# A decode block that streams 561 MB: the output projection's weights as one tile behind the last K load

## The chip, the core and the metric

The kernel runs on one core of a Trainium2 chip. A core has engines that each work through their own list of instructions: TensorE (PE: matmuls, with weight loads shown apart as PEld), VectorE (DVE), ScalarE (ACT), GpSimd (POOL) and SyncE (SP). SyncE issues the transfers from HBM into the on-chip memory SBUF. Matmul results land in PSUM. An instruction waits until those it depends on have signalled, and whatever stands behind it in the same engine's list waits with it. The metric is the device time of one execution in microseconds; smaller is better.

## What is computed

One decoding step for two sequences (B = 2): layer norm, attention against a cache, a residual, and an MLP behind a second layer norm.

```python
q = (layernorm(x) @ wq)                               # 2 x 512 -> 32 heads x 128
scores = einsum("bhqd,bhkd->bhqk", q, k_cache) * 128 ** -0.5
p = softmax(scores)                                   # over 8192 positions
o = einsum("bhqk,bhkd->bhqd", p, v_cache)             # 32 heads x 128
h = x + o.reshape(2, 4096) @ wo                       # wo: 4096 x 512
out = h + gelu(layernorm(h) @ w1 + b1) @ w2 + b2      # w1: 512 x 1792
```

All is float32. The caches k and v are 2 x 32 x 8192 x 128 each, 268 MB each; wq and wo are 8.4 MB, W1 and W2 3.67 MB each.

## The kernel before

The heads are worked off in units. Units 0 to 29 are a pair of heads (a group g = 0 to 14) of one sequence b; units 30 and 31 are heads 30 and 31, each for both sequences. In the text K5 and V5 are the loads of unit 5's keys and values, 8.39 MB each. In a pair's unit, the first head's 8192 positions lie on partitions 0 to 63 and the second's on 64 to 127, 128 positions a partition, so one partition's row in HBM is 64 KB. K30, K31 and V30 come as two loads, one a sequence, and V31 as four.

All of these, wq at the start and the MLP's weights at the end (`wt`) share three slots of 64 KB a partition (`slot()`, the pool `kv`, the tile `kv` in the profile). A load can be issued when the slot's last user is done. The order of the loads is wq, K0, K1, V0, K2, V1, K3 and so on, so a K is two transfers ahead of its use.

For a unit, in four chunks of 32 positions a partition: VectorE multiplies the chunk by q (`multiply`, L183, 128 x 4096), GpSimd adds the upper half of each row to the lower (`halve`, L187, chunks 0 to 2), VectorE sums what is left (`add_up`, L190). `row_max` (L200 or L198) takes the maximum of a partition, TensorE turns it into a row (L202), `all_max` (L207) takes the maximum over a row and matmuls (L211) give it to all partitions. ScalarE's `exps` (L229, L223) writes the probabilities. `values` (L260) multiplies them with V into the PSUM tile `so`, by turns in four groups of rows; `gather` (L266) copies it out and `head_sum` (L274, L276) adds the four groups. A float32 matmul shows as two records.

The output projection runs along with the groups. `load_wo(g)` (L171) loads the group's 256 rows of wo, 0.52 MB in rows of 4 KB a partition, into one of two buffers of the tile `wog`. In the next group's second unit `head_out` scales the pair's result into the tile `orow` with two VectorE operations (L282), `turn` transposes it by two matmuls (L292), `turned` copies it (L296) and adds its product with the group's wo into the PSUM tile `rowacc` by two matmuls (L299). Heads 30 and 31 have their wo rows in a tile of their own and come last: head 30 by `project` (L303); head 31's part is kept apart, and its effect on the layer norm and on the output is computed from `wl`, its 128 rows of wo.

The end, behind V31: the MLP's weights W1 (`w1t`, L372, four loads) and W2 (`w2t`, L376, six loads) go to the slot `wt`. The layer norm's parts are prepared from `rowacc` while V31 is still arriving (L400 to L418); then come V31's matmuls, `gather`, the last head's part (L438, L442), W1's matmuls (L453), the variance (L458), the activation (L468, L470), a transpose (L473), W2's matmuls (L476), a copy (L479) and the store (L480).

The instructions are written in Python's order and a scheduler places them on the engines' lists; it also adds the waits. `behind(m)` is the program's way to say that an engine's next instructions stand behind the instruction m on that engine. Transfers use eight completion semaphores in turn, so that a load may wait for an older one that used the same. Fifteen tiny loads of b1 into the tile `mark` (L321) are spread among the loads of units 24 and on: each waits for the one before.

Of the kernel before, what the change touches and what calls it, by code (L numbers as in the profile page):

```python
# [21 lines left out]
LH = 2  # L22
WARM = 3
MARKS = 15


@with_exitstack
def tile_decode_block(ctx: ExitStack, tc: tile.TileContext, x, k, v, wq, wo, w1, b1, w2, b2, out):
    nc = tc.nc
    B, H, SK, DH = k.shape  # L30
    D = x.shape[-1]
    F = w1.shape[1]
    DC = D // P
# [21 lines left out]
    def slot():  # L55
        return kv.tile([P, ROW], F32, name="kv", tag="kv")
# [41 lines left out]
    y2 = wts.tile([B, D], F32, name="y2", tag="wog")  # L98
# [38 lines left out]
    for j in range(QW // 512):  # L137
        nc.scalar.activation(q2[:, j * 512:(j + 1) * 512], so2[j], AF.Copy)

    QP, S, MX, MT, GM, LT, RL, SS, OP, OT, TP, WO = ({} for _ in range(12))  # L140

    def make_q(g):
        QP[g] = psq.tile([P, B, DH], F32, name="qps")
# [9 lines left out]
    def load(src, i, parts):  # L153
        g, b = units[i]
        h = heads[g][0]
        t = slot()
        if b is not None:
            nc.sync.dma_start(t, src[b, h:h + 2].rearrange("h (p j) d -> (h p) (j d)", j=NS2))
            return t
        tv = t.rearrange("p (b j d) -> p b j d", b=B, d=DH)  # L160
        for e in range(B):
            for s0, n in parts[e]:
                nc.sync.dma_start(tv[:, e, s0:s0 + n],
                                  src[e, h].rearrange("(p j) d -> p j d", j=NS1)[:, s0:s0 + n])
        return t

    def load_wo(g):
        t = wts.tile([P, 2, D], F32, name="wog", tag="wog")
        h = heads[g][0]
        if g < NP:  # L170
            nc.sync.dma_start(t, wo[h * DH:(h + 2) * DH, :].rearrange("(p r) n -> p r n", r=2))  # L171
        else:
            nc.sync.dma_start(t, wo[h * DH:, :].rearrange("(h p) n -> p h n", p=P))
        WO[g] = t

    def chunk(t, c):
        return t[:, c * CH * DH:(c + 1) * CH * DH].rearrange("p (j d) -> p j d", d=DH)
# [11 lines left out]
    def add_up(i, c, t, n):  # L189
        nc.vector.tensor_reduce(S[i][:, c * CH:(c + 1) * CH], chunk(t, c)[:, :, 0:n], axis=AX.X, op=ALU.add)  # L190

    def row_max(i):
        g, b = units[i]
        if not b:
            MX[g] = work.tile([P, B], F32, name="mx")
            MT[g] = psm.tile([1, B, P], F32, name="sm")
        if b is None:
            nc.vector.tensor_reduce(MX[g], S[i].rearrange("p (b j) -> p b j", b=B), axis=AX.X, op=ALU.max)  # L198
# [49 lines left out]
    def values(i, t, e=None):  # L248
        g, b = units[i]
        so = so2[g % 2]  # L250
        if b is not None:
            nu, at, w, cols = NS2 // 4, 0, 16, slice(0, 16)
            p = ptz[b]
        else:
            b, nu, w = e, NS1 // 4, 8
            at, cols = b * nu, ((slice(8, 16), slice(0, 8))[b])
            p = ptz[b][:, nu * (g - NP):nu * (g - NP + 1), :]
        for u in range(nu):
            n = u % NG
            m = nc.tensor.matmul(so[32 * n:32 * n + w], p[:, u, cols], t[:, (at + u) * 512:(at + u + 1) * 512],  # L260
                                 start=(b == 0 and u < NG), stop=(b == B - 1 and u >= nu - NG))
# [16 lines left out]
    def head_out(g):  # L278
        op, rl = OP.pop(g), RL.pop(g)
        if g < NP:  # L280
            for e in range(2):
                m = nc.vector.tensor_scalar(orow[:, :, e * HP:(e + 1) * HP].rearrange("m r p -> m p r"),  # L282
                                            op.rearrange("m (p r) -> m p r", r=2), rl[:, e:e + 1], None,
                                            op0=ALU.mult)
# [4 lines left out]
    def turn(g):  # L289
        TP[g] = psm.tile([P, 2, B], F32, name="sm")  # L290
        for r in range(2):
            nc.tensor.matmul(TP[g][:, r, :], orow[:, r, :], bmask, start=True, stop=True)  # L292

    def turned(g):
        t = work.tile([P, 2, B], F32, name="ot2")
        m = nc.vector.tensor_copy(t, TP.pop(g))  # L296
        w = WO.pop(g)
        for r in range(2):
            nc.tensor.matmul(rowacc, t[:, r, :], w[:, r, :], start=(g == 0 and r == 0), stop=False)  # L299
        return m  # L300

    def project(g):
        nc.tensor.matmul(rowacc, OT.pop(g), WO[NP][:, g - NP, :], start=False, stop=(g == GL - 1))  # L303

    def behind(m):
        return tc.issue_after(m.ins) if m is not None else nullcontext()

    whole = [[(0, NS1)], [(0, NS1)]]
    KT, VT = {0: load(k, 0, whole)}, {}
    first = None  # L310
    for i, (g, b) in enumerate(units):
        if i >= 1:
            VT[i - 1] = load(v, i - 1, whole)
        if i + 1 < NU:
            KT[i + 1] = load(k, i + 1, whole)
        if b == 0 or i == NU - 2:
            load_wo(g)
        if i == NU - 8 and MARKS:
            mark = const.tile([16, 32], F32, name="mark")
            for n in range(1, MARKS + 1):  # L320
                nc.sync.dma_start(mark[:n, :n + 8], b1[:n * 32].rearrange("(p c) -> p c", p=n)[:, :n + 8])  # L321
        kt = KT.pop(i)
        S[i] = work.tile([P, NS2], F32, name="s", bufs=3)
        out_of = g - 1 if b == 1 else NP - 1 if i == NU - 1 else -1
        for c in range(NCH):
            with behind(first):
                m = multiply(i, c, kt)
            first = None
            if c < NCH - 1:
                halve(c, kt)  # L330
            with behind(m):
                if c == 0:
                    if b != 1 and g >= 1:
                        inverse(g - 1)
                    if out_of >= 0:
                        first = head_out(out_of)
                        turn(out_of)
                elif c == 1:
                    if out_of >= 0:
                        first = turned(out_of)  # L340
# [4 lines left out]
            if c == 2 and b == 0 and i >= 1 or c == 2 and i == NU - 2:  # L345
                values(i - 1, VT.pop(i - 1))
                gather(g - 1)
                head_sum(g - 1)
            if c == 2 and i == NU - 1:
                values(i - 1, VT[i - 1], 0)  # L350
        add_up(i, NCH - 1, kt, DH)
        row_max(i)
        if b != 0:
            first = all_max(g)
            exps(g)
            total(g)
        if b == 1:
            values(i - 1, VT.pop(i - 1))
# [9 lines left out]
        nc.sync.dma_start(b2s[e:e + 1], b2[None, :])  # L368
    w1t = wt[:, 0:DC * F].rearrange("p (c f) -> p c f", c=DC)
    w1v = w1.rearrange("(p c) f -> p c f", c=DC)  # L370
    for c in range(DC):
        nc.sync.dma_start(w1t[:, c], w1v[:, c])  # L372
    w2t = wt[:, DC * F:2 * DC * F].rearrange("p (t d) -> p t d", t=FT)
    w2v = w2.rearrange("(p t) d -> p t d", t=FT)
    for t, n in ((0, 4), (4, 4), (8, 2), (10, 2), (12, 1), (13, 1)):
        nc.sync.dma_start(w2t[:, t:t + n, :], w2v[:, t:t + n, :])  # L376

    inverse(GL)
    junk = const.tile([P, 2], F32, name="junk")
    nc.scalar.activation(junk[:, 0:1], LT[GL][:, 0:1], AF.Sqrt)  # L380
    values(NU - 2, VT.pop(NU - 2), 1)
    gather(GL - 1)
    head_sum(GL - 1)
    head_out(GL - 1)
# [6 lines left out]
        at[0] += n  # L391
        return late[:parts, at[0] - n:at[0]]

    wl = WO[NP][:, LH - 1, :]
# [112 lines left out]
```

## Time and profile before

| | |
|---|---|
| time, median of 3 runs | 1316.67 us (1316.04 to 1317.26) |
| the profiled execution, its own time | 1316.34 us |
| its span, first to last instruction | 1314.2 us |
| moved from HBM | 561.02 MB, 427 GB/s over the span |
| busy share of the span | DVE 72%, PE 35%, POOL 33%, ACT 4% |
| mean granted TensorE clock | 0.648 of full speed |

The profile's page cuts the span into 40 slices of 32.9 us and gives for each the busy tenths of each engine, the granted TensorE clock and the bytes moved. A group of instructions is shown by the line, the engine, the operation and the tiles it writes and reads (`kv<-kv,qps`), with its count, busy time, mean time, the idle time ahead of it and what ended that. The chain of waits follows the work that ended last backwards, at each step to what released it. "SPq" rows are issues of transfers by SyncE; a wait row reads "who waited <- for whom: us in total, times, longest".

### The profile page before, as it was taken

What the parts mean: (1) busy time and instruction counts of PE and PEld (TensorE: products, weight loads), DVE (VectorE), ACT (ScalarE), POOL (GpSimd) and SP (SyncE); (2) the same over time, 40 slices, a digit from 0 to 9 for tenths busy, and PEclk for the clock granted to TensorE, in tenths of its full rate; (3) what the DMA queues carried; (4) which work ended last, traced back from release to release, by engine and by line L of the source; (5) the groups of instructions that cost most, each with busy time, mean ns of one, the idle gap of its engine ahead of it and who ended that gap; (6) DMA issues with size and microseconds to landing.
All of it is one profiled execution on the core that took longest, in us unless ns stands there. A gap on an engine that the chain in (4) does not pass through costs nothing.

```text
span 1314.2 us, 6813 instructions
## 1 busy us (share of the span) xinstructions
PE 459.7 (35%) x2829; PEld 148.8 (11%) x2829; DVE 950.5 (72%) x426; ACT 52.3 (4%) x173; POOL 436.6 (33%) x108
## 2 busy tenths in 40 slices
PE   3006133431443324233431343324233431343357
PEld 0001011100111011011100111011011100111113
DVE  1799667688676788767688676788767688669761
ACT  0001000000000000000000000000000000000001
POOL 0444422244422344422244422344422344424230
PEclk9557566575666657666675666656666675666668
DMA  9999999999999999999999999999999999999996
GB/s 415 431 447 409 430 437 435 425 437 431 439 433 423 432 439 428 433 433 431 435 431 431 437 431 433 433 435 427 435 431 429 439 426 436 435 431 432 421 425 266
DMA packets 14403, 561.46 MB, mean 427 GB/s; under 512 B 1809, under 2 KB 1825, under 8 KB 5157
## 3 DMA queue, kind: packets, MB, share of 16 engines
q1 hardware_dynamic: 14368, 561.03, 99.1%
q8 instruction: 22, 0.36, 0.1%
q14 instruction: 9, 0.07, 0.0%
q10 hardware_dynamic: 4, 0.00, 0.0%
HBM read 561.02 MB, written 0.00 MB: 427 GB/s over the span
## 4 chain that ended last, share of the span: by engine, by line
DMA 52%; DVE 28%; PE 13%; issue 3%; ACT 1%; POOL 1%; SPq 0%; DVEq 0%; ACTq 0%
DMA kv<-in_A_k_cache_dram 33%; DMA mark<-in_B_b_dram 17%; DVE kv L183 15%; DVE s L190 11%; PE so L260 11%; DMA kv<-in_A_v_cache_dram 2%; POOL kv L187 1%; PE sm L211 1%; ACT pt L229 1%; DVE orow L282 1%; DVE gm L207 0%; PE sm L202 0%; PE so L453 0%; DVE mx L200 0%; PE po L476 0%
## 5 line engine op out<-in xcount | busy, mean ns | idle before, releaser
L183 DVE TENSOR_TENSOR kv<-kv,qps 128x4096 f32<-128x4096 f32 x128 | 563.7, 4406 | 303.7 <-DMA kv<-in_A_k_cache_dram 294.1
L187 POOL TENSOR_TENSOR kv<-kv 128x2048 f32<-128x2048 f32 x96 | 433.7, 4525 | 828.8 <-DVE kv L183 494.3
L260 PE MATMUL so<-kv,pt 128*16 128x512 f32 (+1 forms) x2048 | 305.5, 734 | 275.6 <-DMA kv<-in_A_v_cache_dram 255.0
L190 DVE TENSOR_REDUCE s<-kv 128x32 f32<-128x2048 f32 (+1 forms) x128 | 356.7, 2806 | 5.9 <-POOL kv L187 5.5
L260 PEld LDWEIGHTS so<-kv,pt 128*16 128x16 f32 (+1 forms) x2048 | 77.2, 111 | 468.2 <-DMA kv<-in_A_v_cache_dram 270.6
L292 PE MATMUL sm<-bmask,orow 4*128 4x2 f32 x60 | 15.1, 352 | 190.5 <-DVE orow L282 190.5
L147 PE MATMUL qps<-q,pick 2*64 2x128 f32 x136 | 18.0, 411 | 150.5 <-DVE kv L183 150.5
L299 PE MATMUL rowacc<-wog,ot 128*2 128x512 f32 x60 | 53.0, 1037 | 49.6 <-DVE ot L296 49.6
L202 PE MATMUL sm<-ident,mx 128*1 128x128 f32 x34 | 10.7, 326 | 135.8 <-DVE mx L200 127.9
L292 PEld LDWEIGHTS sm<-bmask,orow 4*128 4x128 f32 x60 | 13.8, 317 | 193.3 <-DVE orow L282 178.8
L147 PEld LDWEIGHTS qps<-q,pick 2*64 2x64 f32 x136 | 11.8, 203 | 175.9 <-DVE kv L183 157.5
L266 ACT ACTIVATE ss<-so 128x512 f32<-128x512 f32 x17 | 10.1, 597 | 539.9 <-PE so L260 539.9
L216 ACT ACTIVATE nb<-sm 128x2 f32<-128x2 f32 x17 | 2.9, 172 | 675.9 <-PE sm L211 675.9
L229 ACT ACTIVATE pt<-s,nb 64x128 f32<-64x128 f32 x60 | 23.9, 399 | 1.2
L211 PE MATMUL sm<-gm,srow 1*128 1x2 f32 x68 | 16.7, 347 | 8.6 <-DVE gm L207 8.6
L274 PE MATMUL sm<-ss,sel 128*4 128x128 f32 x120 | 15.6, 273 | 10.9 <-ACT ss L266 10.9
L202 PEld LDWEIGHTS sm<-ident,mx 128*1 128x1 f32 x34 | 2.5, 79 | 146.3 <-DVE mx L200 134.3
L207 DVE TENSOR_REDUCE gm<-sm 1x4 f32<-1x256 f32 (+1 forms) x17 | 7.0, 412 | 16.1 <-PE sm L202 16.1
L211 PEld LDWEIGHTS sm<-gm,srow 1*128 1x128 f32 x68 | 15.3, 309 | 13.8 <-DVE gm L207 13.8
L134 PE MATMUL so<-kv,yT 128*2 128x512 f32 x64 | 9.4, 751 | 17.2 <-DMA kv<-in_A_wq_dram 17.2
L299 PEld LDWEIGHTS rowacc<-wog,ot 128*2 128x2 f32 x60 | 5.1, 104 | 72.6 <-DVE ot L296 50.9
L274 PEld LDWEIGHTS sm<-ss,sel 128*4 128x4 f32 x120 | 9.3, 87 | 26.7 <-ACT ss L266 24.7
(98 smaller groups left out, 104.5 us busy)
## 6 DMA issues: line engine op xcount, KB each, us to landing
kv<-in_A_k_cache_dram SPq DMA_DIRECT2D x4, 4096.0 KB
kv<-in_A_v_cache_dram SPq DMA_DIRECT2D x3, 4096.0 KB
wog<-in_A_wo_dram SPq DMA_DIRECT2D x16, 512.0 KB
kv<-in_B_w_dram SPq DMA_DIRECT2D x4, 896.0 KB
kv<-in_A_v_cache_dram SPq DMA_DIRECT2D x1, 2048.0 KB
kv<-in_B_w_dram SPq DMA_DIRECT2D x2, 1024.0 KB
kv<-in_A_v_cache_dram SPq DMA_DIRECT2D x1, 1536.0 KB
kv<-in_B_w_dram SPq DMA_DIRECT2D x2, 512.0 KB
```

The costliest lines, as they stand in the source:

```text
L147: nc.tensor.matmul(QP[g][s * HP:(s + 1) * HP, b], pick[32 * n:32 * n + B, b, :], q2[32 * n:32 * n + B, at:at + DH], start=True, stop=True)
L183: return nc.vector.tensor_tensor(kc, kc, QP[g][:, b, None, :].to_broadcast([P, CH, DH]), op=ALU.mult)
L187: nc.gpsimd.tensor_tensor(kc[:, :, 0:HP], kc[:, :, 0:HP], kc[:, :, HP:DH], op=ALU.add)
L190: nc.vector.tensor_reduce(S[i][:, c * CH:(c + 1) * CH], chunk(t, c)[:, :, 0:n], axis=AX.X, op=ALU.add)
L202: nc.tensor.transpose(MT[g][:, e, :], MX[g][:, e:e + 1], ident)
L211: nc.tensor.matmul(GM[g], srow[:, s, :], gm[:, :, s % n], start=(s == 0), stop=(s == 1))
L229: nc.scalar.activation(ptz[b][q, :, 4 * m:4 * m + 4], s[q], AF.Exp, bias=nb[q, b:b + 1], scale=SCALE, accum_out=lt4[q, m:m + 1])
L260: m = nc.tensor.matmul(so[32 * n:32 * n + w], p[:, u, cols], t[:, (at + u) * 512:(at + u + 1) * 512], start=(b == 0 and u < NG), stop=(b = ...
L274: nc.tensor.matmul(OP[g], sel4[:, :, j], sj, start=(j == 0), stop=(j == 3))
L282: m = nc.vector.tensor_scalar(orow[:, :, e * HP:(e + 1) * HP].rearrange("m r p -> m p r"), op.rearrange("m (p r) -> m p r", r=2), rl[:, e: ...
L292: nc.tensor.matmul(TP[g][:, r, :], orow[:, r, :], bmask, start=True, stop=True)
L299: nc.tensor.matmul(rowacc, t[:, r, :], w[:, r, :], start=(g == 0 and r == 0), stop=False)
```

## The change

wo's rows for heads 0 to 29 are no longer loaded with each group. One load, issued behind K31, brings all 3840 of them as one tile of 7.86 MB (60 KB a partition, in three rows of 20 KB) into one of the three slots; head 30's and 31's rows follow in a tile of their own, `wol`. The results of five groups (ten heads) are kept in `orow`, now laid out per group, and turned together: `turn(j)` makes ten matmuls and `turned(j)` one copy into `oall`, after groups 4, 9 and 14. `project_all` then multiplies all of `oall` with the tile in 30 matmuls, spread over four groups of rows of `so`, gathers them with one copy, and adds them into `rowacc` with one matmul. It is placed in the last unit's third chunk, and the last unit's `row_max` is put behind it on TensorE.

Beside that: K0 comes in two loads of 4.19 MB, W1 in two instead of four, W2 in four (8, 4, 1 and 1 of its 14 parts) instead of six. V30's first half is multiplied after the last unit's softmax, with the second half, and not inside the unit. `add_up` is put behind the multiply of the next chunk. The marks are issued with units 18 to 22, three to a unit.

```diff
@@ tiles @@
-    wts = ctx.enter_context(tc.tile_pool(name="wts", bufs=2))
+    wts = ctx.enter_context(tc.tile_pool(name="wts", bufs=1))
-    orow = const.tile([4, 2, P], F32, name="orow")
-    nc.gpsimd.memset(orow, 0.0)
+    orow = const.tile([4, GP, 2, DH], F32, name="orow")
+    oall = const.tile([P, NP // GP, 2 * GP, B], F32, name="oall")
@@ loads @@
-            nc.sync.dma_start(t, src[b, h:h + 2].rearrange("h (p j) d -> (h p) (j d)", j=NS2))
+            rows = src[b, h:h + 2].rearrange("h (p j) d -> (h p) (j d)", j=NS2)
+            for s0, n in parts:
+                nc.sync.dma_start(t[:, s0 * DH:(s0 + n) * DH], rows[:, s0 * DH:(s0 + n) * DH])
-    def load_wo(g):
...
+    def load_wo():
+        t = slot()
+        tv = t[:, 0:NP * 2 * D].rearrange("p (j c) -> p j c", c=2 * GP * D)
+        nc.sync.dma_start(tv, wo[0:HL * DH, :].rearrange("(j p r) n -> p j (r n)", p=P, r=2 * GP))
+        return tv.rearrange("p j (r n) -> p j r n", n=D)
+
+    def load_last():
+        t = wts.tile([P, LH, D], F32, name="wol", tag="wol")
+        nc.sync.dma_start(t, wo[HL * DH:, :].rearrange("(h p) n -> p h n", p=P))
+        return t
@@ output projection @@
-            for e in range(2):
-                m = nc.vector.tensor_scalar(orow[:, :, e * HP:(e + 1) * HP].rearrange("m r p -> m p r"),
-                                            op.rearrange("m (p r) -> m p r", r=2), rl[:, e:e + 1], None,
-                                            op0=ALU.mult)
-            return m
+            return nc.vector.tensor_tensor(orow[:, g % GP], op[:, None, :].to_broadcast([4, 2, DH]),
+                                           rl[:, :, None].to_broadcast([4, 2, DH]), op=ALU.mult)
+    def turn(j):
+        rows = orow.rearrange("m k e d -> m (k e d)").rearrange("m (p r) -> m r p", r=2 * GP)
+        TP[j] = psm.tile([P, 2 * GP, B], F32, name="sm")
+        for r in range(2 * GP):
+            nc.tensor.matmul(TP[j][:, r, :], rows[:, r, :], bmask, start=True, stop=True)
+
+    def turned(j):
+        return nc.vector.tensor_copy(oall[:, j], TP.pop(j))
+
+    def project_all(wot):
+        so, n = so2[(NP - 1) % 2], 2 * NP
+        for q in range(n):
+            j, r = divmod(q, 2 * GP)
+            m = nc.tensor.matmul(so[32 * (q % NG):32 * (q % NG) + B], oall[:, j, r, :], wot[:, j, r, :],
+                                 start=(q < NG), stop=(q >= n - NG))
+        gather(NP - 1)
+        nc.tensor.matmul(rowacc, sel[:, :B], SS.pop(NP - 1), start=True, stop=False)
+        return m
@@ units @@
-    KT, VT = {0: load(k, 0, whole)}, {}
+    KT, VT = {0: load(k, 0, [(0, NS2 // 2), (NS2 // 2, NS2 // 2)])}, {}
...
+        if i == NU - 2:
+            wot = load_wo()
+            wol = load_last()
+        at = i - (NU - 14)
+        if 0 <= at < 5:
+            for n in range(3 * at + 1, 3 * at + 4):
+                nc.sync.dma_start(mark[:n, :n + 8], b1[:n * 32].rearrange("(p c) -> p c", p=n)[:, :n + 8])
...
             if c >= 1:
-                add_up(i, c - 1, kt, HP)
+                with behind(m):
+                    add_up(i, c - 1, kt, HP)
...
             if c == 2 and i == NU - 1:
-                values(i - 1, VT[i - 1], 0)
+                last = project_all(wot)
         add_up(i, NCH - 1, kt, DH)
-        row_max(i)
+        with behind(last):
+            row_max(i)
@@ end @@
-    for c in range(DC):
-        nc.sync.dma_start(w1t[:, c], w1v[:, c])
+    for c in range(0, DC, 2):
+        nc.sync.dma_start(w1t[:, c:c + 2], w1v[:, c:c + 2])
-    for t, n in ((0, 4), (4, 4), (8, 2), (10, 2), (12, 1), (13, 1)):
+    for t, n in ((0, 8), (8, 4), (12, 1), (13, 1)):
-    values(NU - 2, VT.pop(NU - 2), 1)
+    vt = VT.pop(NU - 2)
+    values(NU - 2, vt, 0)
+    values(NU - 2, vt, 1)
```

More of the change, by code (lines that the diff above doesn't have):

```diff
@@ L97, in tile_decode_block @@
     nc.vector.reciprocal(rs, sd)
-    y2 = wts.tile([B, D], F32, name="y2", tag="wog")
+    y2 = wts.tile([B, D], F32, name="y2", tag="wol")
     nc.vector.tensor_scalar(y2, x2, mv[:, 0:1], rs, op0=ALU.subtract, op1=ALU.mult)
@@ L138, in tile_decode_block @@
         nc.scalar.activation(q2[:, j * 512:(j + 1) * 512], so2[j], AF.Copy)
-    QP, S, MX, MT, GM, LT, RL, SS, OP, OT, TP, WO = ({} for _ in range(12))
+    QP, S, MX, MT, GM, LT, RL, SS, OP, OT, TP = ({} for _ in range(11))
     def make_q(g):
@@ L286, in head_out @@
         OT[g] = work.tile([P, B], F32, name="ot") if g < GL else otz[:, 0:32:16]
         nc.vector.tensor_tensor(OT[g], op, rl, op=ALU.mult)
[L289 to L299, printed above, removed]
+    def turn(j):
[3 more added lines that the diff above has]
+            nc.tensor.matmul(TP[j][:, r, :], rows[:, r, :], bmask, start=True, stop=True)
@@ L300, in turned @@
         return m
     def project(g):
-        nc.tensor.matmul(rowacc, OT.pop(g), WO[NP][:, g - NP, :], start=False, stop=(g == GL - 1))
+        nc.tensor.matmul(rowacc, OT.pop(g), wol[:, g - NP, :], start=False, stop=(g == GL - 1))
     def behind(m):
         return tc.issue_after(m.ins) if m is not None else nullcontext()
-    whole = [[(0, NS1)], [(0, NS1)]]
-    KT, VT = {0: load(k, 0, whole)}, {}
-    first = None
+    whole, full = [[(0, NS1)], [(0, NS1)]], [(0, NS2)]
+    assert NS2 == NCH * CH
@@ L311, in tile_decode_block @@
+    KT, VT = {0: load(k, 0, [(0, NS2 // 2), (NS2 // 2, NS2 // 2)])}, {}
+    mark = const.tile([16, 32], F32, name="mark")
+    first = last = None
     for i, (g, b) in enumerate(units):
         if i >= 1:
-            VT[i - 1] = load(v, i - 1, whole)
+            VT[i - 1] = load(v, i - 1, full if i <= 2 * NP else whole)
         if i + 1 < NU:
[L315 to L320, printed above, removed]
+            KT[i + 1] = load(k, i + 1, full if i + 1 < 2 * NP else whole)
+        if i == NU - 2:
[4 more added lines that the diff above has]
+            for n in range(3 * at + 1, 3 * at + 4):
@@ L336, in tile_decode_block @@
                         first = head_out(out_of)
-                        turn(out_of)
+                        if out_of >= 0 and out_of % GP == GP - 1:
+                            turn(out_of // GP)
                 elif c == 1:
-                    if out_of >= 0:
-                        first = turned(out_of)
+                    if out_of >= 0 and out_of % GP == GP - 1:
+                        first = turned(out_of // GP)
                     if b != 0 and g < GL:
@@ L343, in tile_decode_block @@
             if c >= 1:
-                add_up(i, c - 1, kt, HP)
-            if c == 2 and b == 0 and i >= 1 or c == 2 and i == NU - 2:
+                with behind(m):
+                    add_up(i, c - 1, kt, HP)
+            if c == 2 and (b == 0 and i >= 1 or i == NU - 2):
                 values(i - 1, VT.pop(i - 1))
```

10 lines of the change are left out of this document (2 added, 8 removed).

## The prediction

> **What bounds the kernel now.** The page first: the span, the moved bytes by slice, the queue, and the chain of waits by engine.
>
> ```profile
> span 1314.2 us, 6813 instructions
> ...
> DMA  9999999999999999999999999999999999999996
> GB/s 415 431 447 409 430 437 435 425 437 431 439 433 423 432 439 428 433 433 431 435 431 431 437 431 433 433 435 427 435 431 429 439 426 436 435 431 432 421 425 266
> ...
> q1 hardware_dynamic: 14368, 561.03, 99.1%
> ...
> DMA 52%; DVE 28%; PE 13%; issue 3%; ACT 1%; POOL 1%; SPq 0%; DVEq 0%; ACTq 0%
> ```
>
> 561 MB on one queue, in nines to the last slice: the kernel is a stream, and 561.03 MB at the middle's 433 GB/s would be 1296 us. What is above that is lost at the ends: the slice with 409, and the last one with 266. So next come the stages by time (columns: busy us and count by engine, granted TensorE clock, DMA share, GB/s).
>
> ```profile
> 98.60:131.40 32.80, 20.13 (x135) 6.43 (x135) 30.39 (x14) 3.42 (x10) 13.67 (x3) 0.73 0.97 410
> 580.00:740.00 160.00, 53.11 (x320) 16.97 (x320) 119.46 (x51) 5.46 (x20) 54.42 (x13) 0.65 1.01 434
> 1288.00:1300.00 12.00, 11.31 (x88) 4.62 (x80) 0.55 (x2) 0.60 (x1) 0.00 (x0) 0.90 0.99 407
> 1302.00:1304.00 2.00, 2.00 (x15) 0.47 (x11) 0.16 (x1) 1.72 (x3) 0.00 (x0) 0.50 0.52 204
> 1304.00:1306.00 2.00, 2.00 (x19) 0.50 (x11) 0.54 (x1) 0.00 (x0) 0.00 (x0) 0.98 0.13 49
> 1308.00:1314.20 6.20, 3.14 (x112) 2.87 (x109) 0.29 (x1) 0.00 (x0) 0.00 (x0) 1.00 0.02 3
> ```
>
> The last weights move between 1304 and 1306; I put the landing of the last W2 piece at 1305.3. The span ends 9 us later. The chain of waits in its last stretch (start, us, what) says why:
>
> ```profile
> 1199.60 28.52 DMA kv<-in_A_v_cache_dram
> ...
> 1228.16 9.19 PE so L260 x64
> ...
> 1239.82 4.33 DVE kv L183
> ...
> 1272.19 0.19 DVE mx L198
> ...
> 1276.19 5.59 PE so L260 x32
> ...
> 1287.59 8.45 PE so L260 x64
> ...
> 1300.46 1.37 PE so L453 x6
> ...
> 1301.92 3.46 PE so L453 x24
> ...
> 1307.88 3.31 PE po L476 x112
> 1311.21 0.29 DVE kv L479
> ```
>
> After V of unit 29 lands (1228.16) no transfer ends a wait on this chain. V29's matmuls hold TensorE, the maximum of unit 30 waits behind them, so the multiply of K31 starts at 1239.82; K31 takes VectorE to 1272.38, 32.6 us; its softmax frees V30's second half, and so on to L476 (1311.19). The stream is done 5.9 us before L476 ends (1311.2 - 1305.3). The end belongs to compute that started late, not to the bytes.
>
> **The change, part by part.** *wo out of the stream.* Fifteen 0.52 MB loads ahead of K31 go, and one of 7.86 MB stands behind it. What one costs, from SyncE's issues in order of time:
>
> ```profile
> 264.39 0.33 SPq L158 DMA_DIRECT2D kv<-in_A_k_cache_dram  x1
> ...
> 342.97 0.33 SPq L158 DMA_DIRECT2D kv<-in_A_k_cache_dram  x1
> ...
> 1147.63 0.30 SPq L321 DMA_DIRECT2D mark<-in_B_b_dram  x1
> ...
> 1167.02 0.31 SPq L321 DMA_DIRECT2D mark<-in_B_b_dram  x1
> ...
> 1188.78 0.32 SPq L321 DMA_DIRECT2D mark<-in_B_b_dram  x1
> ```
>
> Each mark is issued when the one before has landed. The first two have one 8.39 MB load between them and are 19.39 us apart (433 GB/s). A group's period holds four such loads and one wo piece: 78.58 us, so the piece takes 78.58 - 4 x 19.39 = 1.0 us; its bytes at 433 GB/s are 1.2, and with that I go on. Everything up to K31 lands 15 x 1.2 = 18.1 us sooner, and the new tile takes 7.86 MB / 433 = 18.2 us behind it: nothing won in bytes. Longer rows may run better: the 7, 8 and 4 KB rows of W1 and W2 move at 407 where K's move at 434, 6% apart. wo goes from 4 KB to 20 KB rows, W1 from 7 to 14, half of W2 from 8 to 16. 6% of 18.1 and of W1 and W2's 18 us is 2.2; I take -1.0 (ends 0 and -2.2), since the period shows no loss on wo. The last two marks, with a wo piece and a load between them, are 21.76 us apart: 2.37 for the piece, 1.2 above its bytes. That is rival B.
>
> The Trainium skill ("DMA: Bandwidth & Descriptors", the section on the anatomy of one DMA, measured there on GpSimd's path) gives each transfer some 2.0 us of fixed cost beside its bytes. By that rule fifteen transfers fewer would be worth an estimated 30 us; the 78.58 us period disagrees.
>
> *First K in two loads.* The start, VectorE, TensorE and SyncE:
>
> ```profile
> 32.06 1.14 PE L147 MATMUL qps<-q,pick 2*64 2x128 f32 x16
> 42.06 8.75 DVE L183 TENSOR_TENSOR kv<-kv,qps 128x4096 f32<-128x4096 f32 x2 [35.56 <-DMA kv<-in_A_k_cache_dram]
> 70.85 0.33 SPq L158 DMA_DIRECT2D kv<-in_A_k_cache_dram  x1
> 99.48 0.33 SPq L158 DMA_DIRECT2D kv<-in_A_v_cache_dram  x1
> 101.31 4.42 DVE L183 TENSOR_TENSOR kv<-kv,qps 128x4096 f32<-128x4096 f32 x1 [0.70 <-DMA kv<-in_A_k_cache_dram]
> ```
>
> V1 is issued at 99.48, when K1's slot comes free, and K2 has landed by 101.31: under 2 us of cover, and the 410 GB/s row follows. Its loss against 434 is 1.8 us at most. With half of K0 at 42.06 - 9.7 = 32.4 and q ready at 33.2, unit 0 ends near 62 instead of 70.85, unit 1 (28.6 us) near 91, and V1 has 10 us of cover. I take -1.2 (ends 0 and -1.8).
>
> *o by fives, and the projection in one go.* Per pair two L282, a copy and 2 + 2 matmuls become one VectorE operation; each fifth pair adds ten transposing matmuls and a copy. These were beside the stream:
>
> ```profile
> L292 PE MATMUL sm<-bmask,orow 4*128 4x2 f32 x60 | 15.1, 352 | 190.5 <-DVE orow L282 190.5
> DVE kv L183 <- DMA kv<-in_A_k_cache_dram: 294.1, 29, 35.6
> SPq L321 <- DMA mark<-in_B_b_dram: 173.7, 14, 21.0
> SPq L372 <- DMA kv<-in_A_v_cache_dram: 12.7, 4, 4.5
> ```
>
> Twenty records (a matmul is two) at 0.25 us (15.1 / 60) are 5.0 us against the 4.4 us multiply above them: the new copy holds VectorE under 1 us, three times, in units where it waits 10 us for K (294.1 / 29). Nothing. The cover would be gone only if a unit took 10 us longer. The marks move to units 18 to 22; SyncE waited 173.7 us on them at full rate, so that moves nothing either. W1 and W2 in fewer issues wait for V31's pieces as L372 does now; W1's first is issued when V31's first half lands, 10 us of V31 being still queued.
>
> *The tail.* Take 18.1 + 1.2 = 19.3 off the chain: V29 lands at 1208.9, K31's multiply starts at 1220.5, VectorE is done with it at 1253.1. Now the stream backwards: W1 and W2 (7.34 MB at 407) end 18.0 us after V31, so V31 ended at 1287.3, V30 19.4 before at 1267.9; less 2.2 these are 1285.1 and 1265.7. The wo tile lands 20.6 before V30's end, at 1245.1; project_all (30 matmuls, 60 records like L260's 64 in 9.19) holds TensorE to 1254, row_max(31) behind it, softmax 3.8 later (1276.19 - 1272.38) at 1258. V30 comes last: its second half runs 1265.7 to 1271.3, the step to V31's matmuls is 5.8 (1287.59 - 1281.78), 8.45 more give 1285.6, and V31's last piece is there. That is 10 us sooner than 1296.04. L453 could start 4.4 later at 1290, but W1's second half lands at 1294.1: 16 records (2.3) and the activation (2.5) bring L476 to 1298.9, and 3.31 to 1302.2. W2's last piece lands at 1305.3 - 2.2 = 1303.1. The stream decides; 8 records (0.24) and 3.0 (1314.2 - 1311.21) follow.
>
> Two slots are dearer: the new tile waits for VectorE on K30, done before K31's start at 1220.5, while K31's bytes last to 1208.9 + 19.4 = 1228.3; and V31 waits for K31 (1253.1) instead of V29, with V30 in flight to 1265.7. 12 us of cover; gone, it costs what is missing. Behind the tile's issue SyncE holds V30, V31, W1 and W2; behind project_all's wait for the tile TensorE holds row_max(31) and V30's matmuls.
>
> *TensorE's clock.* The table's clock column is 0.50 while L453 runs and 1.00 under L476. With waits between TensorE's bursts L476 may run at half: 3.31 becomes 6.6, ending at 1298.9 + 6.6 = 1305.5 instead of 1303.3, +2.2; at most +3.3. I take +0.8, nearer the 1.00 row as the warm-up matmuls stay. The Trainium skill ("TensorE: Matmul & The Clock Gate", part 1) says the clock falls to half after an idle window of about 3.4 us: a rule against this change, which puts idle there; by it the time is rival A's.
>
> **Sum.** -5.9 (chain no longer last) + 0.24 - 1.0 - 1.2 + 0.8 = -7.1. The profiled execution took 1316.34 around a span of 1314.2, the median is 1316.67; 1316.67 - 7.1 = 1309.6.
>
> **Rivals.**
> A. Half clock at the end: -7.1 - 0.8 + 3.3, about -4.6, 1312.1. For it: the 0.50 row; against: the 1.00 row. Chance 0.17.
> B. A wo piece costs 1.2 above its bytes, as between the last two marks: 15 x 1.2 = 18 more, 1291.6. Against: the period, where four loads and a piece fit their bytes. Chance 0.02.
> C. Slower: V31 waits for K31's slot and the stream runs dry. A hole opens when VectorE ends K31 past 1265.7, and the time is above 0.2% slower when the hole is over 7.1 + 2.6, past 1275.4, 22 us later than worked out. If K31 keeps its place behind V29's matmuls and the whole 19.3 us is lost again (1272.4) with another 8 (VectorE's and GpSimd's waits in that unit), the hole is 14.7: 1324.3. For it: K31's 32.6 us have waits in them; against: 12 us of cover. Chance 0.08.
> D. The end stays: project_all waits for the wo tile and row_max(31) for it, so softmax comes not at 1258 but after V30, 7.1 past 1265.7, and L476 comes last again: 1316.7. For it: the new order on TensorE; against: some 15 us between 1258 and that point. Chance 0.07.
>
> **Numbers.** Forecast 0.66. 0.2% (2.6 us) is what a measurement of this kernel can tell. Faster: 0.66 + 0.17 + 0.02 = 0.85; same 0.07; slower 0.08. Range: best, both stream terms at their ends and full clock, -5.7 - 2.2 - 1.8 = -9.7, 1307.0; worst of A, neither term and +3.3, -5.7 + 3.3 = -2.4, 1314.3. That leaves out B, C, D.
>
> **What the profile would show.** Right: 19.3 us between K issues without a wo piece; V1 issued near 91 and the fourth slice back at 430; K31's first multiply near 1221; L476's counterpart waiting for W2's transfers; the bytes ending near 1303. Wrong: a slice under 420 between 1250 and 1290 (C), a 0.50 clock in the last 8 us (A), that last group ended by VectorE's transpose again (D).

## The result, and the profile after

| | before | after |
|---|---|---|
| median of the runs | 1316.93 us (4 runs, 1316.04 to 1317.26) | 1309.02 us (4 runs, 1308.87 to 1309.61) |
| ratio, after to before | | 0.9942, 95% interval 0.9925 to 0.9959 |
| span of the profiled execution | 1314.2 us | 1306.9 us |

The changed kernel is 7.9 us faster by the medians and 7.3 us by the two spans; the forecast was 1309.6 with 7.1 us less. Its lines have moved by up to 16: the multiply is L188, V's matmuls L265, project_all L304, W1's matmuls L469, the activation L486 and W2's matmuls L492.

These are the page's lines of the changed kernel that answer to those shown of the kernel before: the moved bytes by slice and the queue.

```profile
span 1306.9 us, 6750 instructions
...
GB/s 403 435 445 422 442 429 436 431 434 437 428 439 426 437 428 438 425 445 424 440 427 439 428 435 432 432 437 426 439 426 439 426 441 426 439 422 433 425 431 335
...
q1 hardware_dynamic: 12176, 561.03, 99.4%
```

The same 561.03 MB move in 2192 packets fewer, and the last slice moves 335 GB/s where it moved 266: the bytes now reach nearly to the end. The stretches by time show it closer (columns as in the prediction: busy us and count by engine, clock, DMA share, GB/s).

```profile
98.60:131.40 32.80, 15.98 (x121) 4.60 (x114) 29.04 (x11) 0.60 (x1) 13.51 (x3) 0.73 1.03 445
580.00:740.00 160.00, 45.21 (x304) 14.52 (x304) 121.06 (x46) 5.46 (x20) 56.05 (x13) 0.63 1.00 432
1277.00:1282.00 5.00, 5.00 (x28) 1.32 (x32) 0.17 (x1) 0.00 (x0) 0.00 (x0) 0.50 1.00 418
1286.00:1298.00 12.00, 11.31 (x90) 5.23 (x83) 1.03 (x6) 2.34 (x4) 0.00 (x0) 0.72 0.99 417
1300.00:1302.00 2.00, 1.78 (x64) 1.69 (x64) 0.16 (x1) 0.00 (x0) 0.00 (x0) 1.00 0.50 194
1302.00:1304.00 2.00, 1.78 (x56) 1.19 (x48) 0.15 (x1) 0.00 (x0) 0.00 (x0) 1.00 0.10 39
```

The fall of the rate that stood at 204 and 49 GB/s in the kernel before (1302 to 1304, 1304 to 1306) stands at 194 and 39 two microseconds sooner. L492's 112 records now run inside it, where L476's ran behind it, and take 3.61 us instead of 3.31, with two waits for W2 among them. The middle runs at 432 as it did at 434. So the stream ends some 2 us sooner, and what followed it has shrunk by 5. The chain of waits, in its last stretch:

```profile
1178.45 29.18 DMA kv<-in_A_v_cache_dram
...
1207.67 9.07 PE so L265 x64
...
1217.14 49.25 DMA kv<-in_A_v_cache_dram
...
1266.44 5.26 PE so L265 x32
...
1277.50 9.95 PE so L265 x64
...
1292.10 1.48 PE so L469 x6
...
1293.65 4.06 PE so L469 x24
...
1300.22 3.61 PE po L492 x112
```

The chain before went from V29 over K31's VectorE work to the end without a transfer. Now it follows V30's transfer until 1266.4: K31 and its softmax have dropped off it. From there it is TensorE's work on V30, V31 and W1, and L492 begins at 1300.22 while W2 is still landing.

### The profile page after: what moved, and what is told of

Same layout as the page of the kernel before. It is cut to its first block, busy times and chain, and to the rows that moved or that the text cites. A ratio compares the mean times of both kernels' runs of the same rounds, so it can differ in the third digit from the quotient of the medians.

```text
span 1306.9 us, 6750 instructions
## 1 busy us (share of the span) xinstructions
PE 414.2 (32%) x2831; PEld 144.5 (11%) x2831; DVE 948.2 (73%) x399; ACT 52.9 (4%) x174; POOL 436.2 (33%) x107
## 3 DMA queue, kind: packets, MB, share of 16 engines
q1 hardware_dynamic: 12176, 561.03, 99.4%
## 4 chain that ended last, share of the span: by engine, by line
DMA 45%; DVE 31%; PE 17%; POOL 5%; ACT 2%; issue 1%; DVEq 0%; SPq 0%; POOLq 0%; ACTq 0%
DMA kv<-in_A_k_cache_dram 38%; DVE kv L188 16%; DVE s L195 13%; PE so L265 12%; DMA kv<-in_A_v_cache_dram 6%; POOL kv L192 5%; DMA kv<-in_A_wq_dram 2%; PE sm L216 1%; ACT pt L234 1%; PE sm L295 1%; PE so L135 1%; DVE gm L212 0%; PE so L469 0%; PE sm L207 0%; DVE mx L205 0%
## 5 line engine op out<-in xcount | busy, mean ns | idle before, releaser
L188 DVE TENSOR_TENSOR kv<-kv,qps 128x4096 f32<-128x4096 f32 x128 | 564.1, 4409 | 285.3 <-DMA kv<-in_A_k_cache_dram 259.1
L265 PE MATMUL so<-kv,pt 128*16 128x512 f32 (+1 forms) x2048 | 304.0, 730 | 263.2 <-DMA kv<-in_A_v_cache_dram 242.6
L265 PEld LDWEIGHTS so<-kv,pt 128*16 128x16 f32 (+1 forms) x2048 | 77.0, 111 | 453.6 <-DMA kv<-in_A_v_cache_dram 257.7
L304 PE MATMUL so<-kv,oall 128*2 128x512 f32 x60 | 8.8, 724 | 16.8 <-DMA kv<-in_A_wo_dram 16.8
L234 ACT ACTIVATION_READ_ACCUMULATOR pt<-s,nb 64x1 f32 x60 | 11.1, 185 | 0.0
```

Source lines behind the costliest of these rows:

```text
L188: return nc.vector.tensor_tensor(kc, kc, QP[g][:, b, None, :].to_broadcast([P, CH, DH]), op=ALU.mult)
L234: nc.scalar.activation(ptz[b][q, :, 4 * m:4 * m + 4], s[q], AF.Exp, bias=nb[q, b:b + 1], scale=SCALE, accum_out=lt4[q, m:m + 1])
```

## The experiments

Twelve more kernels or copies were run, each beside the kernel before. Ratios are to the kernel before; the changed kernel has 1309.02 in its first runs and 1308.87 when run again. It ran beside the sums set free, V30's first half inside the last unit and the candidate; the other edits are compared with its first runs. Edits that change nothing gave 1308.8 to 1309.0 on two chips, so differences to the changed kernel under some 0.3 us say nothing.

**K0 whole again.**

```diff
-    KT, VT = {0: load(k, 0, [(0, NS2 // 2), (NS2 // 2, NS2 // 2)])}, {}
+    KT, VT = {0: load(k, 0, full)}, {}
```

> The changed kernel with K0 in one load again. Theory: VectorE starts at 42 instead of 32.7, K1's slot is free at 99.5 instead of 90.4, when K2 (100.1) is about to land: the stream stops for the time from an issue to its first bytes and everything behind is 1.0 to 2.5 us later: 1310.0 to 1311.5. Rival (the stream has cover there anyway): within 0.3 us.

Measured: 1311.07 us (6 runs), ratio 0.9949 (0.9936 to 0.9963): 2.05 us slower than the changed kernel. First its rows in order of time (SyncE's issue of V1, VectorE on K2 and K3) and its stretch from 98.6 to 200, then the same of the changed kernel.

```profile
99.50 0.33 SPq L161 DMA_DIRECT2D kv<-in_A_v_cache_dram  x1
...
100.57 4.40 DVE L188 TENSOR_TENSOR kv<-kv,qps 128x4096 f32<-128x4096 f32 x1
...
142.27 4.42 DVE L188 TENSOR_TENSOR kv<-kv,qps 128x4096 f32<-128x4096 f32 x1 [11.48 <-DMA kv<-in_A_k_cache_dram]
```

```profile
98.60:200.00 101.40, 34.99 (x223) 12.06 (x223) 78.86 (x33) 6.15 (x20) 39.46 (x9) 0.63 0.99 424
```

```profile
90.39 0.33 SPq L161 DMA_DIRECT2D kv<-in_A_v_cache_dram  x1
...
100.11 4.42 DVE L188 TENSOR_TENSOR kv<-kv,qps 128x4096 f32<-128x4096 f32 x1 [8.59 <-DMA kv<-in_A_k_cache_dram]
...
140.12 4.42 DVE L188 TENSOR_TENSOR kv<-kv,qps 128x4096 f32<-128x4096 f32 x1 [10.91 <-DMA kv<-in_A_k_cache_dram]
```

```profile
98.60:200.00 101.40, 31.45 (x219) 10.39 (x215) 79.68 (x30) 2.73 (x10) 40.61 (x9) 0.65 1.00 433
```

With K0 whole, V1 is issued 9.1 us later, when K2 is about to land, and K3's multiply starts 2.15 us later. 9 GB/s less over 101.4 us are 101.4 x 9 / 433 = 2.1 us: the whole loss lies there, and it stays to the end.

**The kernel before, with K0 in two loads alone.**

```diff
-                nc.sync.dma_start(t, src[b, h:h + 2].rearrange(...))
+                rows = src[b, h:h + 2].rearrange(...)
+                for s0, n in ((0, NS2 // 2), (NS2 // 2, NS2 // 2)) if src is k and i == 0 else ((0, NS2),):
+                    nc.sync.dma_start(t[:, s0 * DH:(s0 + n) * DH], rows[:, s0 * DH:(s0 + n) * DH])
```

> The kernel before with one part of the change alone: K0 in two loads of 4.19 MB, VectorE starting on the first. Theory: the late chain at the end hangs on V29's landing, and V29's landing on the stream, so the whole end moves with the stream: 1.2 us faster as forecast, up to 2.1 by the run with K0 whole; 1314.6 to 1315.7. Rival: the end belongs to VectorE's chain alone and a fuller stream at the start changes nothing, within 0.3 us of the kernel before. Signs for the theory: V1 issued near 91 us instead of 99.5, V29's landing earlier by the same amount as the end.

Measured: 1315.25 us (12 runs, 1314.18 to 1319.28) against 1318.40 of the kernel before (23 runs, 1315.46 to 1321.11), ratio 0.9979 (0.9967 to 0.999): 1.3 to 4.4 us faster. The chain of this kernel:

```profile
1197.15 30.08 DMA kv<-in_A_v_cache_dram
...
1286.09 8.35 PE so L262 x64
...
1306.29 3.31 PE po L478 x112
```

V29 lands at 1227.23 instead of 1228.12, 0.9 us sooner, and L476's counterpart starts 1.6 us sooner. So a chain that is last and hangs on a landing passes on what the stream gains there. The same amount at both was expected; the rest of the 1.6 lies behind that landing, and one profile of each doesn't show why. The medians' 3 us say no more than the sign, because this kernel and the kernel before spread over 5 us.

**W2 cut short, in both kernels.** The last six of W2's fourteen parts are not loaded, and their matmuls read parts that are there; part of W2 is left out of the result. In the changed kernel:

```diff
-    for t, n in ((0, 8), (8, 4), (12, 1), (13, 1)):
+    for t, n in ((0, 7), (7, 1)):
...
-    ... w2t[:, t, n * P:(n + 1) * P],
+    ... w2t[:, t % 8, n * P:(n + 1) * P],
```

> The changed kernel without the last six of W2's 14 parts: they are not loaded, and their matmuls read the first parts again (this leaves part of W2 out of the output). The stream ends 1.57 MB or 3.9 us sooner, at full count of matmuls. If the stream alone decides the end now: -3.5 us or more. If TensorE's chain behind V31 is equally late (it starts L492 at 1300.22 and needs 3.3 us for 112 records, to 1303.5, against 1303.83 measured): -0.3 us. I expect the second, -0.3.

The same in the kernel before:

```diff
-    for t, n in ((0, 4), (4, 4), (8, 2), (10, 2), (12, 1), (13, 1)):
+    for t, n in ((0, 4), (4, 2), (6, 1), (7, 1)):
```

> The kernel before with the last six of W2's fourteen parts not loaded; their matmuls read the first parts again, so this leaves out part of W2 and 1.57 MB of the stream (some 3.6 us at its end), and no other work. Theory: the stream had been done 5.9 us before the last matmuls, which wait for a late chain on VectorE and TensorE, so the time stays: 0 plus or minus 0.5 us. Rival: the last bytes decide there too, and it ends up to 3.6 us sooner. In the changed kernel the same edit gave 1.1 us.

Measured in the kernel before: 1318.01 us (12 runs) against 1318.40, ratio 1.0002 (0.999 to 1.0014): nothing. One stretch of its stream, and its chain:

```profile
1302.00:1304.00 2.00, 2.00 (x24) 0.68 (x20) 0.16 (x1) 1.40 (x2) 0.00 (x0) 0.50 0.00 0
```

```profile
1286.32 9.99 PE so L260 x64
...
1302.51 4.08 PE so L453 x24
...
1309.09 3.31 PE po L476 x112
```

No byte moves after 1302, and L476 comes no sooner (1309.09, with V31's matmuls 1.5 us longer than in the kernel before): the prediction's first part, that the end belonged to compute, is shown. Measured in the changed kernel: 1307.88 us (5 runs), ratio 0.9924 (0.991 to 0.9938), 1.1 us faster. Its chain:

```profile
1278.78 8.76 PE so L265 x64
...
1299.43 3.31 PE po L492 x112
```

With the last bytes gone, TensorE's chain alone ends L492 at 1302.74, against 1303.83. Only 0.3 us was expected. L492 does take 0.3 us less without its waits for W2 (3.31 against 3.61); the other 0.8 is its sooner start, mainly because W1's matmuls and those just ahead of them take 0.9 us less there, and whether that belongs to the missing bytes is not shown. In the changed kernel the stream and that chain end within about a microsecond of each other, and neither alone is worth more.

**wo's tile ahead of K31.**

```diff
+        if i == NU - 2:
+            wot = load_wo()
         if i + 1 < NU:
             KT[i + 1] = load(k, i + 1, ...)
         if i == NU - 2:
-            wot = load_wo()
             wol = load_last()
```

> The changed kernel with the one wo tile issued ahead of K31 instead of behind it. Same bytes, same transfers, same instructions; K31 lands 18.2 us later (7.86 MB at 433 GB/s) and V30 and all behind it where they did. Theory (the end moved because K31's chain starts sooner): K31's multiply starts near 1236 instead of 1219.1, its softmax comes near 1269 instead of 1257, after V30 has landed (1266.4), so V30's 64 records end near 1278 instead of 1271.7 and all behind them 6 to 7 us later: 1315 to 1316, the gain gone. Rival (fewer and larger transfers are what is won): no change, 1309.

Measured: 1312.33 us (5 runs, 1311.57 to 1314.10), ratio 0.9959 (0.9945 to 0.9974): 3.3 us slower than the changed kernel, half of what the theory said. The chain:

```profile
1208.62 27.15 DMA kv<-in_A_k_cache_dram
1235.79 4.42 DVE kv L188
...
1273.37 3.66 PE so L265 x32
...
1282.83 9.18 PE so L265 x64
...
1303.86 3.31 PE po L493 x112
```

K31's multiply starts at 1235.79, when K31 lands, 16.6 us later than in the changed kernel, and the chain runs over VectorE to the end as it did before. Against the kernel before it starts 4.0 us sooner (1239.82) and its last matmuls start 4.0 us sooner (1307.88). The two agree in size and not step by step: the last maximum is ready 6.5 us sooner (1265.72 against 1272.19), and part of that is lost again behind it. Against the changed kernel the 16.6 us become 3.6 at the last matmuls (1303.86 against 1300.22). Some 8 of them are slack there, since its softmax is done near 1258 and V30 lands at 1266.4. The last unit's maximum no longer stands behind project_all on TensorE, which saves some 5.5 (in the changed kernel it is ready at 1248.8 and goes to TensorE at 1254.3). V30's and V31's matmuls take 2.4 us less here (3.66 + 9.18 against 5.26 + 9.95) and W1's some 0.7. Against that, matmuls of V30's first half fall between the softmax's steps and cost 3.4.

**The tile in fifteen loads with rows of 4 KB**, in the same place of the queue.

```diff
-        nc.sync.dma_start(tv, wo[0:HL * DH, :].rearrange("(j p r) n -> p j (r n)", p=P, r=2 * GP))
+        for j in range(NP // GP):
+            for r in range(0, 2 * GP, 2):
+                nc.sync.dma_start(tv[:, j, r * D:(r + 2) * D], wov[:, j, r * D:(r + 2) * D])
```

> The changed kernel with the wo tile, at the same place, in 15 loads of 0.52 MB with rows of 4 KB instead of one of 7.86 MB with rows of 20 KB. Theory (a wo piece costs its bytes, and its short rows a little): +0.7 us, between 0 and +2.2. Rival (each transfer costs 1.2 us or more beside its bytes): +17 us or more, 1326.

Measured: 1309.89 us (5 runs), ratio 0.994 (0.9926 to 0.9954): 0.87 us slower. **W1 in four and W2 in six loads again:**

```diff
-    for c in range(0, DC, 2):
-        nc.sync.dma_start(w1t[:, c:c + 2], w1v[:, c:c + 2])
+    for c in range(DC):
+        nc.sync.dma_start(w1t[:, c], w1v[:, c])
...
-    for t, n in ((0, 8), (8, 4), (12, 1), (13, 1)):
+    for t, n in ((0, 4), (4, 4), (8, 2), (10, 2), (12, 1), (13, 1)):
```

> The changed kernel with W1 in four loads and W2 in six again (rows of 7, 8, 4 and 2 KB instead of 14, 16, 8 and 2 KB). By the forecast's term for longer rows (2.2 us at most over 25 MB, of which W1 and W2 are 7.3) 0.3 us slower, 0 to 0.9; by the rival that row length costs nothing there, within 0.2, and it could win a little, as W1's matmuls can begin on a quarter.

Measured: 1309.03 us (5 runs, 1308.95 to 1309.29), ratio 0.9928 (0.9913 to 0.9943): 0.0 to 0.2 above the changed kernel, which can't be told from nothing; 0.3 was expected. Its stretch that answers to the changed kernel's row of 1286 to 1298:

```profile
1286.00:1298.00 12.00, 11.15 (x86) 5.21 (x81) 1.17 (x6) 2.34 (x4) 0.00 (x0) 0.72 1.00 408
```

408 GB/s with short rows, 417 with long ones: 12 x 9 / 417 = 0.3 us in this stretch. So the rows' length and the number of loads together are worth 0.9 us for wo and 0 to 0.3 for W1 and W2. The chain with the fifteen loads (L492 is L495 there) ends with the stream:

```profile
1286.86 15.97 DMA kv<-in_B_w_dram
1302.87 1.30 PE po L495 x40
```

**What should be free.** Without the marks:

```diff
-        if 0 <= at < 5:
+        if 0 <= at < 5 and not MARKS:
```

> The changed kernel without the fifteen tiny marks; the array mark stays unwritten and unused. Theory: SyncE's waits on them lie beside a full stream, so nothing changes: 0 plus or minus 0.4 us against the changed kernel. Rival: they set which completion semaphore a load takes, so that without them a load waits for an older one: 1 us or more slower, with a slice of the stream under 420 GB/s.

Measured: 1308.82 us (5 runs), ratio 0.9927 (0.9912 to 0.9942): no difference. With the sums free to go ahead of the multiplies:

```diff
             if c >= 1:
-                with behind(m):
-                    add_up(i, c - 1, kt, HP)
+                add_up(i, c - 1, kt, HP)
```

> The changed kernel with the scheduler free again to put a chunk's sum ahead of the next chunk's multiply, as before the change. The forecast gave this edit no price. K31 took VectorE 29.4 us with it and 32.6 us in the kernel before. Theory: undone, K31 takes some 3 us longer, V31 is issued 3 us later with 13 us of cover left, and the softmax comes near 1261 with V30's last piece landing at 1266: 0 plus or minus 0.4 us. Rival: those 3 us are on the path, since VectorE's first two units set when V1 is issued: 1 to 3 us slower.

Measured: 1308.94 us (5 runs, 1308.75 to 1309.08), ratio 0.9937 (0.9924 to 0.9951): no difference. VectorE's last sum of K31 ends at 1251.39 there, 1244.77 + 6.62, and V31's transfer follows:

```profile
1219.77 4.41 DVE kv L188
...
1244.77 6.62 DVE s L195 x2
...
1252.77 33.06 DMA kv<-in_A_v_cache_dram
```

With V30's first half inside the last unit again:

```diff
                 last = project_all(wot)
+                last = values(i - 1, VT[i - 1], 0)
...
-    values(NU - 2, vt, 0)
```

> The changed kernel with V30's first half multiplied inside the last unit again, behind the projection and ahead of the last unit's maximum on TensorE. Theory: V30's first half lands near 1257, its 32 matmul records take 3.6 us, and the maximum comes near 1261 instead of 1254.3; the softmax is done near 1265, still ahead of V30's last piece at 1266.4: 0 plus or minus 0.4 us. Rival: the maximum is on the path as in the kernel before (where a maximum waited behind V's matmuls): 2 us or more slower, with the stream done before the last matmuls.

Measured: 1309.02 us (5 runs), ratio 0.9938 (0.9925 to 0.995): no difference, although V30's first half stands ahead of the last unit's maximum on TensorE (from 1257.0, 3.8 us; the row is in the last section). These three edits have slack around them, as costed or, for the sums, as found.

**A candidate, and the changed kernel again.** The candidate has no marks, V30's first half inside the last unit and W1 in four loads.

> A candidate: no marks, V30's first half inside the last unit (TensorE busy up to V30's last piece, so its second half could run at full clock, 3.7 us instead of 5.2), W1 in four loads. Theory: the last bytes of W2 land near 1303.3 whatever TensorE does, so at best 0.3 us faster than the changed kernel: 1308.7 to 1309.2. Rival: TensorE's chain sets the end, and 1.5 us less in it brings up to 1.1 us, as leaving out a part of W2 did.

> The changed kernel unchanged, on the chip of the next three, to compare them on: 1309.0 as measured, within 0.5 us. Theory: a kernel whose end is set by the stream repeats within 1 us, while the kernel before, whose end is set by a late chain on TensorE with its changing clock, spreads over several us. Rival: the spread of the kernel before belongs to the chip and shows here too.

Measured: the candidate 1308.77 us (5 runs, 1308.61 to 1309.63), ratio 0.9937 (0.9925 to 0.995); the changed kernel again 1308.87 us (5 runs, 1308.73 to 1308.90), ratio 0.9936 (0.9924 to 0.9949). They cannot be told apart. V30's second half was hoped to run at full clock in the candidate and did not: it took 6.4 us, not 3.7. L492 still starts sooner there, at 1299.62, and waits for W2: a sooner start on TensorE is not worth anything while W2's last bytes land when they do. The second kernel's expectation held too: it spread over 0.2 us, and the kernel before over 4.3 us on the same chip at the same time (9 runs, 1315.93 to 1320.19).

## Why the prediction was right, step by step

*The chain is no longer last (-5.9): right, and shown from both sides.* Cutting W2 short does nothing to the kernel before; moving the tile ahead of K31 brings the late chain back. The times on the way were near. V29 lands at 1207.6 (1208.9 predicted), K31's multiply starts at 1219.1 (1220.5), its sums end by 1248.5 (1253.1):

```profile
1219.14 4.40 DVE L188 TENSOR_TENSOR kv<-kv,qps 128x4096 f32<-128x4096 f32 x1
...
1228.72 0.18 DVE L298 COPY oall<-sm 128x20 f32<-128x20 f32 x1 [0.45 <-PE sm L295]
...
1245.53 8.85 PE L304 MATMUL so<-kv,oall 128*2 128x512 f32 x60 [16.84 <-DMA kv<-in_A_wo_dram]
...
1248.50 0.28 DVE L203 TENSOR_REDUCE mx<-s 128x2 f32<-128x128 f32 x1
```

The tile is there at 1245.5 (1245.1 predicted) and project_all takes 8.85 us where 9.19 was taken from V's matmuls. The turn of ten costs VectorE 0.45 us of waiting, under the 1 us that was called nothing.

*K31 in 32.6 us: too long by 3.* It takes 29.4. The prediction listed the new order of the sums but gave it no price, and kept the old duration. Undone, VectorE takes K31 from 1219.77 to 1251.39, 31.6 us, so that the order is worth 2.3 of the 3.2; the time stays. The omission cost nothing only because V31 had cover to spare: it is issued by 1250.3 (the changed kernel's sums end at 1248.5, and the issues follow) with V30 in flight to 1266.4, 16 us where 12 were worked out. Rival C did not come near.

*A wo piece costs its bytes, 1.2 us: 1.36.* VectorE's start on K, twenty loads of K apart, in the kernel before and in the changed one:

```profile
221.57 4.42 DVE L183 TENSOR_TENSOR kv<-kv,qps 128x4096 f32<-128x4096 f32 x1 [9.77 <-DMA kv<-in_A_k_cache_dram]
...
1010.86 4.42 DVE L183 TENSOR_TENSOR kv<-kv,qps 128x4096 f32<-128x4096 f32 x1 [9.59 <-DMA kv<-in_A_k_cache_dram]
```

```profile
217.69 4.42 DVE L188 TENSOR_TENSOR kv<-kv,qps 128x4096 f32<-128x4096 f32 x1 [9.74 <-DMA kv<-in_A_k_cache_dram]
...
993.42 4.42 DVE L188 TENSOR_TENSOR kv<-kv,qps 128x4096 f32<-128x4096 f32 x1 [9.58 <-DMA kv<-in_A_k_cache_dram]
```

789.29 us for ten groups with a piece each against 775.73 without: 1.36 a piece, 0.16 above its bytes. The single period that the prediction read gave 1.0, and the last two marks gave 2.4; one period is too short for such a reading. Rival B (2.4 a piece) is refuted.

*Longer rows (-1.0, ends 0 and -2.2): right in size.* Undone for wo they cost 0.87 us, for W1 and W2 0 to 0.3. The bound was read too wide: the 407 GB/s of the stretch with W1 and W2 was taken for a price of their short rows, 6%, but with 14 and 16 KB rows it is 417, so that rows are 2% of it and the rest has another cause. The 0.16 us a piece in the last paragraph would make 15 x 0.16 = 2.4 us; 0.87 of it is shown to be rows and count. Whether the rest is a price of standing between loads of K and V was not tried.

The Trainium skill ("DMA: Bandwidth & Descriptors", the section on the anatomy of one DMA, on GpSimd's path) has some 2.0 us of fixed cost for a transfer. Fourteen transfers more (the prediction counted fifteen, without the tile's own load) cost 0.87 us here, 0.06 us each, short rows included: in this queue, which always holds further loads, no such cost is seen, and the measurement decides.

*K0 in two loads (-1.2, ends 0 and -1.8): mis-sized.* It measured 2.05 us in the changed kernel, beyond the end. VectorE starts at 32.7 and V1 is issued at 90.39, as predicted. The bound of 1.8 came from one slice of the kernel before, where V1 was issued 1.8 us ahead of K2's landing (99.48 and 101.31). With wo's pieces out of the stream K2 lands sooner, by 100.57 at the latest, and V1 at 99.50 would have had 1.1 us at most: the loss without this edit would have grown. The two parts of the change interact, and the prediction priced this one in the old stream. In the kernel before, the same edit brings V29's landing only 0.9 us forward, and K3's multiply 0.8 (141.93 against 142.74). With K2 landing at 100.1, as in the changed kernel, V1 had 0.6 us of cover in the kernel with K0 whole and 2.15 were lost; 1.8 us of cover lost 0.8. Both add up to some 2.7 us, an estimate of the cover that an issue needs here. The sign that was named, the fourth slice at 430, is not to be seen (422): slices of 33 us are too short for it. The stretch from 98.6 to 200 shows it, 433 against 424.

*TensorE at half clock (+0.8): the place was wrong, and it has no price at the end.* L492 runs at full clock (1.00 in the rows of 1300 to 1304), so rival A did not come at that place. The half clock fell on V31's matmuls (0.50 from 1277 to 1282: 9.95 us for 64 records, 8.45 in the kernel before) and on W1's (1.48 + 4.06 against 1.37 + 3.46). L492 so started at 1300.2 instead of 1298.9, and with the 3.31 us of the kernel before it would have ended at 1303.5. But the weight loads of its last eight records (PEld) wait for W2's last piece:

```profile
1303.36 0.16 PEld L492 LDWEIGHTS po<-kv 128*32 128x32 f32 x8 [0.24 <-DMA kv<-in_B_w_dram]
```

That piece is there at 1303.36 (1303.1 worked out), and the eight records take 0.47 us from it to the end at 1303.83 (0.24 worked out). These two make up the 0.5 us over the 1303.34 that the forecast had without its clock term, and the clock has no part in them.

*The stream decides: right, but narrowly.* In the rerun of the changed kernel and most experiments the chain's last transfer is W2, with the last 48 of L492's records behind it. In the first profile the chain of waits runs over TensorE, yet its last eight records too wait for W2; TensorE alone would have been done 0.3 us sooner. Rival D (the end stays) was refuted: the softmax had 8 us of slack, and V30's first half could be put ahead of it without any loss.

The sum was -7.1, the spans say -7.3. That they are so near is in part luck. The chain's -5.9 stands. The stream ends some 2 us sooner, where 2.2 was put down: K0's 2.05 is not all a gain over the kernel before, because removing wo's pieces first made that loss larger; what the kernel before had to win there was 0.9, and the rows gave another 0.9 to 1.2. The clock's 0.8 was not needed and covered the 0.5 by which the landing and the last eight records were put too short. K31's 3 us lay where there was slack.

## What to carry to other kernels

When the bytes end before the work does, look for the work that hangs on the last big transfer and ask what may be loaded behind it: bytes that are needed late and briefly (here a projection of 8.85 us) belong behind bytes that start a long chain (here 29 us on VectorE). The gain ends where the stream's end and the next chain meet, so work out both ends before trimming either. Parts of a change that act on the same queue are to be priced in the stream as the other parts leave it.

## What the hardware showed beside that

*The kernel that ended on a late chain spread, the one that ends with its stream did not; why is open.* The kernel before spread over 4.3 and 5.7 us in its last two sets of runs, the changed kernel over 0.7 and 0.2. V31's 64 records alone took 8.35, 8.45, 8.76, 9.18, 9.95 and 9.99 us in the profiles shown here, with half clock in the first 4.5 us of the 9.95. That is 1.6 us between them, not 5. A run's mean clock does not order the times either: the kernel before took 1316.49 us at 0.642 and 1320.81 at 0.643. The runs of 1320 us were not traced, so that the clock makes the spread is not shown.

*TensorE's clock halved inside a wait of 3 us.* V30's second half should have run at full clock once its first half stood closer ahead of it. It did not; in the kernel with V30's first half inside the last unit the stretches and TensorE's two bursts are:

```profile
1257.00:1260.60 3.60, 3.60 (x33) 1.37 (x32) 0.00 (x0) 0.00 (x0) 0.00 (x0) 1.00 1.01 437
1260.60:1263.70 3.10, 1.51 (x12) 0.90 (x8) 0.41 (x1) 1.39 (x6) 0.00 (x0) 1.00 1.06 449
1263.70:1266.70 3.00, 0.00 (x0) 0.00 (x0) 0.17 (x1) 1.05 (x2) 0.00 (x0) 0.72 0.94 404
1266.70:1268.00 1.30, 1.29 (x8) 0.28 (x12) 0.00 (x0) 0.00 (x0) 0.00 (x0) 0.50 0.94 403
```

```profile
1257.01 3.81 PE L265 MATMUL so<-kv,pt 128*8 128x512 f32 x32
...
1266.71 6.14 PE L265 MATMUL so<-kv,pt 128*8 128x512 f32 x32 [3.03 <-DMA kv<-in_A_v_cache_dram]
```

TensorE was busy to 1260.6, had small matmuls to 1263.7 (1.51 of 3.10 us) and nothing for 3.0 us (1263.7 to 1266.7). The second half took 6.1 us instead of 3.8. The gap's mean of 0.72, with 1.00 ahead of it and 0.50 behind it, puts the fall of the clock some 1.3 us into the gap, near 1265.0. The Trainium skill ("TensorE: Matmul & The Clock Gate", part 1) gives an idle window of about 3.4 us that is free-running and does not start anew with a kernel. Here the 3.4 us ahead of the fall still hold some 1.0 us of matmuls (0.60 from 1261.63 and 0.38 from 1263.30), and the clock fell all the same: the measurement decides.
